# Emitting the first convolution of a state-space / attention kernel in a searched order, with engines chosen along with it

## Chip, cores, metric

One core of a Trainium2 chip. The metric is the device time of one execution in microseconds (us). All quoted runs are of the fast state, unless marked. Engines: PE is TensorE, DVE is VectorE, ACT is ScalarE, POOL is GpSimd.

## The reference

Four layers on `x` of 2048 x 512 in bf16: convolution, attention, the same convolution, the same attention, each behind a layer norm and with a residual.

```python
def _A_ref(u, A_re, A_im, B_re, B_im, C_re, C_im, log_dt, Dskip):   # cut
    P = jnp.exp((dt * A)[:, :, None] * l[None, None, :])            # 512 x 128 x 2048
    K = jnp.einsum("dn,dnl,dn->dl", Cc, P, dt * Bc).real            # the long kernel
    Yf = rfft(pad(u)) * rfft(pad(K))                                # length 4096
    return irfft(Yf)[..., :L] + u * Dskip

def _B_ref(x, wqkv, wo):     # cut: 32 heads of 16, 8 keys at distance 0, 2, .., 14
    attn = softmax(where(mask, q . k * scale, -1e9))
    return (attn . v) @ wo

x = x + _A_ref(_layernorm(x), ...);  x = x + _B_ref(_layernorm(x), wqkv, wo)
x = x + _A_ref(_layernorm(x), ...);  x = x + _B_ref(_layernorm(x), wqkv, wo)
```

## The kernel before

The long kernel `K` is contracted on PE from eight tables of powers, which DVE builds by doubling: two products and a sum for each level. Transforms are matmuls; between two of them data is turned (transposed), by DMA or by PE. In the first conv all this is emitted by hand. (Names in the profiles of a conv: `Ttab` and `Y2tab` are tables, `Z` the first half of a transform and `zt` its turned copy, `xc` or `sp_u` the spectrum of the input, `Kt` or `sp_k` that of the kernel, `pa` and `pb` their products, `vp` the inverse in PSUM and `VT` its copy, `X` the rows on which the layers work, handled in four quarters. In an attention layer `xn` is the normed input, `xnT` its turned copy, and `L` (in the code `Lf`) holds the terms of the softmax.)

```python
class Tables:                                   # cut
    def base(self, T, hc, x0=0, x1=2, levels=range(4)):
        for lev in levels:
            nc.vector.tensor_tensor(dst, src, mult(0), ALU.mult)       # products
            nc.vector.tensor_tensor(tb[...], src, mult(1), ALU.mult)
            nc.vector.tensor_tensor(d, d, tb[... ::-1 ...], ALU.add)   # the level's sum
    def high(self, T, hc):                      # the same once more, 128 x 2048

# kernel_and_first_conv: steps are lists of closures, `play` emits lists in turn
play(t[:2], ks[5:6], [store], ks[6:9], t[2:3], p[:2], v[:1], t[3:4], p[2:3], v[1:2], p[3:], v[2:], [fin],
     ks[9:], t[4:], [lambda: residual(dc)])     # t tables, ks kernel spectrum, p products, v inverses
```

The three later stages are already emitted in a listed order, with fixed engines:

```python
def sums():                                     # b_layer, softmax: three adds on DVE
    den = tree("sm_s", ALU.add, F32)
    nc.vector.reciprocal(rdb, den)
    nc.vector.tensor_tensor(Lf, Lf, spread(rdb), ALU.mult)

def mm(j=j, wide=wide, begin=True, fts=range(4)):   # b_layer, output block (cut)
    if begin:
        nc.tensor.matmul(ps, ident[:], X[:, j, :], start=True, stop=False)     # residual
    for ft in fts:
        nc.tensor.matmul(ps, box["oT"][...], wo_t[:, ft, :], start=False, stop=(ft == 3))
es.append(pl.op("A", 0.48, lambda ...: evac(...), a, ...))                     # copy on ACT
```

## Time and profile before

558.31 us median (557.58 to 560.0, 4 runs); the profiled execution has a span of 560.9 us. I cut it at seven events: the first table seed (36.3 us), the end of the last joined spectrum product of the first conv, the first q·k product of the first attention layer, the end of its last value product, the end of the last spectrum product of the second conv, the first q·k product of the second attention layer, the end of its last value product. Busy us of the three engines in each stage, from the view by windows:

| stage | length | PE | DVE | ACT |
|---|---|---|---|---|
| tables and first conv | 199.65 | 124.5 | 181.8 | 120.2 |
| entry to attention 1 | 17.87 | 13.8 | 14.3 | 11.9 |
| body of attention 1 | 103.40 | 94.6 | 92.8 | 59.1 |
| join and second conv | 64.27 | 55.7 | 46.7 | 58.4 |
| entry to attention 2 | 25.14 | 17.5 | 20.2 | 13.7 |
| body of attention 2 | 101.05 | 93.6 | 92.0 | 48.0 |
| tail | 13.20 | 8.2 | 0.0 | 4.9 |

Read it by asking which engine fills its row: DVE the first, PE and DVE the bodies, ACT (91%) the second conv. The lines themselves are in the prediction.

### The profile page before, as it was taken

The page shows a single profiled execution, that of the slowest core. Times are in us where ns is not written, and L with a number is a line of the kernel's source. Part 1 is how long each engine was busy: PE and PEld are TensorE (multiplying, and loading weights), DVE is VectorE, ACT ScalarE, POOL GpSimd, SP SyncE. Part 2 cuts the span into 40 slices and gives each one's busy share as a digit, 9 for nine tenths or more (in the row PEclk, how much of TensorE's full clock was granted, in tenths as well). Part 3 has the DMA queues.
Part 4 walks back from the last instruction along what each step waited for, and adds up shares of the span by engine and source line. Part 5 has one row for each costly group of instructions (what it writes and reads, how often), then busy time and mean ns, then how long its engine had stood idle before and what let it go on. Part 6 is the DMA issues. An engine that isn't in the chain of part 4 may idle for free.

```text
span 560.9 us, 11633 instructions
## 1 busy us (share of the span) xinstructions
PE 412.3 (74%) x4838; PEld 236.1 (42%) x4838; DVE 477.0 (85%) x805; ACT 343.8 (61%) x516; POOL 12.9 (2%) x62
## 2 busy tenths in 40 slices
PE   1201465585586678879999789868994998996996
PEld 0100333363454447543446234455763533552353
DVE  5999999999979959787799998537999587999890
ACT  4999765435355546865666147999974756642253
POOL 0000000000000001200000000000000000000000
PEclk9999998789799879999999799979998899998799
DMA  8200175646453474621010412615330500123141
GB/s 272 111 1 0 31 129 108 96 113 114 78 151 51 95 152 122 223 57 47 16 51 30 104 37 39 250 69 88 71 71 0 76 28 16 50 69 71 34 131 76
DMA packets 91808, 46.65 MB, mean 83 GB/s; under 512 B 80882, under 2 KB 87026, under 8 KB 90474
## 3 DMA queue, kind: packets, MB, share of 16 engines
q1 hardware_dynamic: 90170, 45.51, 34.2%
q8 instruction: 38, 0.62, 0.5%
q10 hardware_dynamic: 1584, 0.39, 0.3%
q14 instruction: 16, 0.13, 0.1%
HBM read 15.77 MB, written 8.13 MB: 43 GB/s over the span
## 4 chain that ended last, share of the span: by engine, by line
PE 38%; DVE 35%; ACT 14%; DMA 6%; issue 6%; SPq 1%; DVEq 0%; ACTq 0%
PE ps_qk L1072 8%; PE po L1232 5%; PE ps_v L1092 4%; DVE prod L1216 3%; PE Lp L1133 3%; DVE Ttab L579 3%; DMA zt<-Z 2%; PE ps_o L1286 2%; DVE ln_st_b L148 2%; DVE Ttab L547 2%; DVE Y2tab L579 2%; DVE prod L1123 2%; ACT Z L808 2%; DVE tb L544 2%; DVE Ttab L543 2%
## 5 line engine op out<-in xcount | busy, mean ns | idle before, releaser
L1123 DVE TENSOR_TENSOR prod<-qT,kT 128x2048 bf16<-128x2048 bf16 (+1 forms) x80 | 75.5, 1006 | 14.8 <-ACT kT L1077 8.7
L1216 DVE TENSOR_TENSOR prod<-VX,L 128x2048 bf16<-128x2048 bf16 (+2 forms) x96 | 77.0, 863 | 1.4 <-PE Lp L1133 0.9
L1232 PE MATMUL po<-prod,sb_ident 128*128 128x512 bf16 x224 | 59.0, 411 | 10.4 <-DVE prod L1216 9.5
L1072 PE MATMUL ps_qk<-xnT,wqk 128*128 128x512 bf16 x256 | 64.1, 385 | 3.1 <-ACT qT L1077 1.4
L213 PE MATMUL psA<-X,sb_F 128*128 128x128 bf16 x128 | 12.2, 238 | 43.3 <-ACT X L638 33.3
L213 PEld LDWEIGHTS <-sb_F 128*128 128x128 bf16 x256 | 19.0, 112 | 59.0 <-issue 58.1
L1232 PEld LDWEIGHTS <-sb_ident 128*128 128x128 bf16 x224 | 22.6, 104 | 41.1 <-issue 11.3
L1072 PEld LDWEIGHTS <-wqk 128*128 128x128 bf16 x256 | 22.7, 99 | 34.0 <-issue 14.2
L607 ACT CAST KTq<-psk 128x1024 bf16<-128x1024 f32 (+1 forms) x9 | 8.3, 917 | 42.5 <-PE psA L238 41.0
L1092 PE MATMUL ps_v<-wv,xnT 128*128 128x256 bf16 x256 | 33.2, 278 | 1.0 <-ACT xnT L1051 0.8
L216 ACT CAST Z<-psA 128x1024 bf16<-128x1024 f32 (+1 forms) x32 | 29.0, 970 | 8.0 <-PE psA L213 8.0
L597 PE MATMUL psk<-Ttab 128*32 128x64 bf16 x1024 | 22.5, 206 | 13.9 <-issue 13.9
L1077 ACT CAST qT<-ps_qk 128x512 bf16<-128x512 f32 x32 | 18.8, 588 | 18.0 <-PE ps_qk L1072 18.0
L1286 PE MATMUL ps_o<-wo_t,oT 128*128 128x512 bf16 x112 | 29.7, 386 | 0.0
L1252 ACT CAST ot<-po 128x1024 bf16<-128x1024 f32 x14 | 13.6, 1014 | 25.8 <-PE po L1232 25.8
L1133 PE MATMUL Lp<-prod,sb_bones 128*32 128x512 bf16 x256 | 28.1, 394 | 1.0 <-DVE prod L1123 0.8
L310 ACT CAST VT<-psA 128x512 bf16<-128x512 f32 x32 | 17.2, 589 | 17.5 <-PE psA L276 16.3
L1092 PEld LDWEIGHTS <-xnT 128*128 128x128 bf16 x256 | 23.8, 99 | 9.6 <-issue 4.5
L579 DVE TENSOR_TENSOR Ttab<-Ttab,MPA 128x2048 bf16<-128x2048 bf16 (+2 forms) x20 | 27.7, 1431 | 0.0
L1097 ACT CAST VX<-ps_v 128x512 bf16<-128x512 f32 x32 | 18.8, 587 | 14.3 <-PE ps_v L1092 14.3
L579 DVE TENSOR_TENSOR Y2tab<-Ttab,MPB 128x6144 bf16<-128x6144 bf16 (+1 forms) x13 | 27.2, 2119 | 0.0
L1077 ACT CAST kT<-ps_qk 128x512 bf16<-128x512 f32 x32 | 18.8, 587 | 11.7 <-PE ps_qk L1072 11.6
(203 smaller groups left out, 1018.0 us busy)
## 6 DMA issues: line engine op xcount, KB each, us to landing
X<-in_A_u_dram SPq DMA_DIRECT2D x8, 512.0 KB, 5.2
kt_scratch<-Kt SPq DMA_DIRECT2D x4, 1024.0 KB, 5.1
Kt<-kt_scratch SPq DMA_DIRECT2D x4, 1024.0 KB, 8.9
out_dram<-X SPq DMA_DIRECT2D x4, 512.0 KB, 2.7
k_scratch<-KTq SPq DMA_DIRECT2D x7, 256.0 KB, 2.4
KT<-k_scratch SPq DMA_DIRECT2D x7, 256.0 KB, 2.9
VX<-VX SPq DMA_DIRECT2D x4, 448.0 KB, 3.7
kT<-kT SPq DMA_DIRECT2D x8, 192.0 KB, 2.1
```

What stands on the lines that cost most here:

```text
L213: nc.tensor.matmul(o, F1[:, j, r, :], rhs_j(j), start=True, stop=not dk)
L216: nc.scalar.copy(Z[:, 0:n // 8, :, jq * 32:(jq + 1) * 32].rearrange("p g r k -> p r g k"), ps[:, :, 0:n // 8, :])
L579: nc.vector.tensor_tensor(dst, src.to_broadcast([128, q, n, 2 * EYB]), mm.to_broadcast([128, q * n, EYB, 2]), ALU.mult)
L597: nc.tensor.matmul(o.rearrange("e (s i) -> e s i", s=2), xs, T[:, 1:3, h, m // 2, :, t], start=(m == 0), stop=False, skip_group_check=True)
L1072: nc.tensor.matmul(ps[:], wqk[:, ct, f0:f0 + 128], xnT[:, 4 * s:4 * s + 4, ct, :], start=(ct == 0), stop=(ct == 3))
L1077: nc.scalar.copy((qT, kT)[which][fp][:, f2, o:o + 512], box.pop(("qk", which, fp, f2, s))[:])
L1092: nc.tensor.matmul(ps[:, jj].rearrange("p t h d -> p (t h d)"), xnT[:, j + jj, ct, :], wv[:, ct, fp * 256:(fp + 1) * 256], start=(ct == 0) ...
L1123: nc.vector.tensor_tensor(pr[:, 0:n2], qT[fp][:, a:a + n2, j0 * 128:j0 * 128 + 1024], kT[fp][:, a:a + n2, c0:c0 + 1024], ALU.mult)
L1133: nc.tensor.matmul(Lp[r0:r0 + 32, w // 4, :], bones[:, w % 4, :], pr[:, f2 - a, hb * 512:(hb + 1) * 512], start=(n == 1), stop=(n == 4), s ...
L1216: nc.vector.tensor_tensor(p2[:, 0:nj].rearrange("p j t d h -> p (j t) d h"), VX[:, fp, NV + a:NV + a + nj].rearrange("p j (t d h) -> p (j ...
L1232: nc.tensor.matmul(po[:, c:c + 512], ident[:], p2[:, k + j:k + j + 2].rearrange("p j t d h -> p (j t d h)"), start=(n == 1), stop=(n == W))
L1286: nc.tensor.matmul(ps, box["oT"][:, ft // 2, j, ft % 2, :], wo_t[:, ft, :], start=False, stop=(ft == 3))
```

## The change

The intent: write the first conv, too, as operations with dependencies, search an order for all engines together offline, and let the search choose the engine of small pieces of work. An operation may have two ways; the way whose numbers appear in the order is built.

```diff
+ORDERS = [ "33 58 34 59 35 60 36 61 37 62 ...",        # first conv: new; three more, all searched anew
 class Plan:
+    def either(self, name, *ways):
+        for k, way in enumerate(ways):
+            self.way = name, k
+            out.append(way())
     def run(self):
         order = [int(i) for i in ORDERS[Plan.turn].split()]
+        taken = {self.ops[i][2] for i in order}
+def moved(pl, nc, name, us, slow, fn, *after, **needs):   # a PSUM copy on ACT or on DVE
+    return pl.either(name, lambda: pl.op("A", us, lambda: fn(nc.scalar.copy), *after, **needs),
+                     lambda: pl.op("V", slow, lambda: fn(nc.vector.tensor_copy), *after, **needs))
+    def sum_mm(self, ps, ident, hc, lev, k):               # Tables: a sum as two matmuls with the identity
+            self.nc.tensor.matmul(o, ident, a[:, i * n:i * n + n], start=True, stop=False)
+            self.nc.tensor.matmul(o, ident, b[:, i * n:i * n + n], start=False, stop=True)
+        psA = es.enter_context(tc.tile_pool(name="k_psA", bufs=3, space=PSUM))      # was 2
+                t = pl.either(("turn", kind, dc, i), by_dma, by_pe) if both else by_dma()
+            return o, pl.either(("join", dc, c), lambda: [], lambda: pl.op("V", 0.7, join, o))
-                den = tree("sm_s", ALU.add, F32)
+                    for w in range(W):                      # softmax sums: eight matmuls into PSUM
+                        nc.tensor.matmul(ps[:], ident[:], Lf[:, :, w, :], start=(w == 0), stop=(w == W - 1))
+            a = pl.either(("den", fp, j0), on_tensor, on_vector)
+        def added(j, ps):                                   # output block: residual as an add on DVE
+            nc.vector.tensor_tensor(X[:, j, :], ps, X[:, j, :], ALU.add)
```

(Cut to its core. A "join" is the subtract and add that turn the two complex products into one spectrum on DVE; without it the inverse has 16 matmuls instead of 8.)

## The prediction

> **What bounds the kernel now.** I first read the engine totals and the 40 slices of the page, to see which engine is full where.
>
> ```profile
> PE 412.3 (74%) x4838; PEld 236.1 (42%) x4838; DVE 477.0 (85%) x805; ACT 343.8 (61%) x516; POOL 12.9 (2%) x62
> ...
> PE   1201465585586678879999789868994998996996
> ...
> DVE  5999999999979959787799998537999587999890
> ```
>
> No engine is full all the time: DVE (second row of digits) is full in the first third, where PE is half used, and PE is dense from the middle on. So I cut the span into stages and asked for the busy time of each engine in each stage (window, its length, then PE, weight loads, DVE, ACT, POOL, clock, DMA share):
>
> ```profile
> 36.00:236.00 200.00, 124.50 (x2875) 84.89 (x2874) 182.15 (x242) 120.51 (x158) 7.48 (x13) 0.91 0.48 100
> 236.00:250.00 14.00, 9.98 (x86) 6.12 (x87) 13.18 (x69) 8.92 (x18) 0.00 (x0) 1.00 0.27 67
> 250.00:345.00 95.00, 87.86 (x543) 40.56 (x542) 84.24 (x107) 50.23 (x79) 2.39 (x20) 0.96 0.19 47
> 345.00:425.00 80.00, 68.69 (x584) 45.34 (x583) 59.79 (x135) 72.23 (x121) 0.00 (x0) 0.96 0.40 100
> 440.00:548.00 108.00, 100.59 (x642) 47.16 (x641) 94.36 (x132) 53.84 (x80) 2.39 (x20) 0.95 0.23 57
> 548.00:561.00 13.00, 7.87 (x38) 3.29 (x35) 0.00 (x0) 4.69 (x8) 0.00 (x0) 0.94 0.21 82
> ```
>
> Four regimes. The tables and first conv (36 to 236 us) are DVE's: 182 of 200 us, PE and ACT near 60%. The bodies of the two attention layers (250 to 345, 440 to 548) are shared by PE (93%) and DVE (88%). The join of the first attention layer to the second conv and that conv (345 to 425) is ACT's, 90%. The last 13 us have no DVE at all: PE, then the last store.
>
> Next, the waits of DVE in the first window, because idle time of the bound engine is what an order can win:
>
> ```profile
> DVE pa L283 <- ACT Kt L239: 9.3, 4, 3.8
> DVE pa L283 <- issue: 2.7, 2, 2.2
> DVE pa L283 <- ACT X L329: 2.2, 1, 2.2
> ```
>
> 14.2 us, all before one instruction, the spectrum product: written in its place in program order, it stands at the head of DVE's queue while table work behind it could run. Last, the time order of one table sum, and the end of the chain of waits:
>
> ```profile
> 177.39 1.23 DVE L558 TENSOR_TENSOR Ttab<-Ttab,MHA 128x2048 bf16<-128x2048 bf16 x1
> 178.53 1.22 DVE L559 TENSOR_TENSOR tx<-Ttab,MHB 128x2048 bf16<-128x2048 bf16 x1
> 179.78 1.22 DVE L561 TENSOR_TENSOR Ttab<-Ttab,tx 128x2048 bf16<-128x2048 bf16 x1
> 180.93 3.42 DVE L579 TENSOR_TENSOR Ttab<-Ttab,MPA 128x2048 bf16<-128x2048 bf16 x2
> ```
>
> ```profile
> 529.88 3.45 PE po L1232 x16
> ...
> 554.62 0.22 PE ps_w L1284
> 554.84 0.45 PE ps_w L1286 x2
> 555.29 0.02 issue
> 555.31 0.59 ACT X L1414
> 555.90 0.04 issue
> 555.95 0.61 PE ps_w L1286 x2
> 556.55 0.02 issue
> 556.58 0.59 ACT X L1414
> ```
>
> Starts, not durations, count on DVE: L558 to L559 is 1.14 us, L559 to the dependent L561 1.25 us. In the tail every output block pays a 0.22 us residual matmul (L1284), and the last block waits for the copy of the one before.
>
> **What the Trainium skill says.** "VectorE: DVE Perf Modes", Side-by-side: where the cycles go for N=2048 bf16, gives about 1224 ns for a two-per-cycle operation; the trace has 1.22 us, so a table sum is already at its best rate and can only be moved. "TensorE: Matmul & The Clock Gate", Wait, 56ns, not 53.3ns?, gives a start-to-start of 215.7 ns at N=512 and 55.6 ns at N=128 once warm; 3.45 us over 16 matmuls is 0.216 us each, in agreement. "Perfetto Trace Analysis", Optimizing Scalar/DVE Operations, gives DVE a higher access overhead on PSUM than on SBUF, and ScalarE a lower one on PSUM. The trace agrees: 128x512 out of PSUM is 682 ns on DVE (VT, L881) and 588 ns on ACT (qT, L1077), so a copy given to DVE costs slightly more engine time than it saves on ACT. "PSUM — Partial Sum Buffer", Specifications (TRN2), allows a VectorE instruction one tensor from PSUM; the new add takes ps_o from PSUM and X from SBUF, so it is in order.
>
> **The change, part by part.** I counted the two built programs' instructions by engine, tile and size, and priced the difference with the durations above. Total counts hardly move (DVE 805 before and after), so this is a change of order and of engine.
>
> Tables and first conv. (a) Four of eight 128x2048 high sums and one 128x1024 sum leave DVE: 4 x 1.25 + 0.7 = -5.7 us DVE. They come back as 36 matmuls of N=512 (7.8 us PE) and 8 copies of 128x1024 plus 2 of 128x512 (8 x 1.02 + 2 x 0.59 = 9.3 us ACT), on engines at about 60%. (b) The first half table is no longer built in two halves: some -0.7 us. (c) Seven spectrum pairs are joined on DVE instead of four: 3 x 0.77 = +2.3 us; one VT copy +0.7. (d) Thirteen turns leave the DMA queue for PE and ACT (13 x 1.02 = 13.3 us ACT, about 6 us PE), which shortens the chain from Z to product; three PSUM buffers for two. DVE work: -5.7 - 0.7 + 2.3 + 0.7 = -3.4 us. ACT reaches some 143 of 200, PE some 136: neither becomes the bound. (e) In DVE's new list the products stand behind table work (table 5 is nearly done before the second group of products, and statistics fill the last spectrum's latency), so most of the 14.2 us should close; I take 10. Stage: -13 us.
>
> Entry of the first attention layer (236 to 250): PE waits for the norms there. DVE keeps its statistics; I take -1.
>
> Attention bodies. Seven of eight softmax sums go to PE: each takes 0.42 + 0.29 + 0.29 = 1.0 us off DVE, -7.0 us in all, and adds 8 matmuls of N=128, 0.45 us, 3.1 us PE in all. The waits of DVE for the exponential, 4.6 us in two waits, go because the list puts products between the steps. Fourteen q and k copies come to DVE (14 x 0.6 = +8.5) where it waited 14.5 us for them. Nineteen of 32 residual matmuls go (-19 x 0.216 = -4.1 us PE) and become adds on DVE (19 x 0.62 = +11.8, most in the tail and in the join where DVE is idle; about six within the second body). Four of eight turns of xn on PE go to DMA (-1.8 us PE). First body: DVE 84.2 - 3 + 3.7 = 85, PE about 89, of 95: the floor is near 89, and I take half of the room, -3. Second: DVE 94.4 - 4 + 4.9 + 3.7 = 99, PE about 101, of 108: I take -4.
>
> Join and second conv (345 to 425), ACT's. Quarter 2 goes to batch statistics: four squares with their reads, 4 x 0.92 = -3.7, four reads of the sum -0.8; five output copies become adds, -3.0; two more norms +1.6. In the conv: five 128x1024 and two 128x512 Z copies, three zt copies and one X copy leave (-5.3 - 1.2 - 3.1 - 0.6), thirteen VT copies arrive (+7.8). ACT: -8.3 us of 72. DVE takes some +4 us and has 20 us free. The rest is latency (a 5 us transposing DMA, a 10 us wait for the first xc), so I take 5 of the 8. Turn to the second layer (425 to 440): four norms leave DVE, -1.
>
> Tail. Eight output blocks after the last value product save 8 x 0.22 = 1.7 us, and the last block's wait for a copy goes, 0.6: -2.
>
> Sum: -13 - 1 - 3 - 4 - 5 - 1 - 2 = -29. The stages are not independent and a searched order meets real latencies, so I keep 26: 558.4 - 26 = **532 us**.
>
> **Rivals.** (1) Only the moved work counts and the idle time merely changes place: the offline order rests on durations that the chip does not keep, and DVE's queue is strict, so a late copy blocks as before. Then -3 in the first stage, -4 in the join, -2 in the tail, about nothing in the bodies: some 549 us. For it: the three later stages already had listed orders and still hold 20 us of DVE waits. Against it: the first stage was hand ordered and holds 14.2 us on one line. (2) The moves make ACT the bound in the first stage: 120 us rises by 23 to 143 of about 187, in bursts where sums, turns and copies meet; table sums would then wait on ACT and give the 5.7 us back. Against it, the new list puts two to four DVE operations behind each moved sum. Result near 541. (3) The order closes nearly everything: first stage 187 - 4, bodies at the floors 89 and 101, all 8 us of the join: about 520.
>
> **Range and chances.** I hold the centre at 532, between (2) and (3); 8 times in 10 it should be between 522 and 545, the upper end being half of the reordering lost. Faster by over 2% means under 547.2: only a full rival (1) misses it. 0.91 faster, 0.08 within 2%, 0.01 slower.
>
> **What would show it.** Right: the last joined product before about 223 us instead of 236; the waits of DVE before the products, 14.2 us, under 5; DVE busy in that stage about 179; no wait for the exponential; ACT in the join stage about 64; no residual matmul on the chain of waits in the last 8 blocks, and a chain that ends in a DVE add. Wrong: waits of DVE on the copies of moved sums, bodies still 95 and 108 us long, or a first stage over 195 us.

## The result

530.43 us median (529.37 to 532.08, 4 runs) against 558.31: ratio 0.9499, 95% interval 0.9466 to 0.9532. A ratio is the mean time of one kernel's fast runs over that of the other's fast runs in the same rounds, so it is not quite the ratio of the medians. The profiled execution has a span of 528.9 us, 32.0 us less than the one of before (medians: 27.9). The profiled execution of the kernel before took 562.7 us by the device's clock, more than any of its four timed runs, so the changes by stage below are together some 4 us too large. A later set of runs on a chip where the kernel before took 560.2 us gave 529.6 us and 0.9456.

The page of the changed kernel, engine totals and DVE's 40 slices:

```profile
PE 404.1 (76%) x4929; PEld 238.6 (45%) x4943; DVE 475.5 (90%) x803; ACT 339.2 (64%) x505; POOL 12.9 (2%) x62
...
DVE  4999999999999998749899998889989497999995
```

DVE's busy time hardly moved (477.0 to 475.5 us): it is the same work in a shorter span. The digits of the first conv (fourth to sixteenth slice) are now 9s but for the last. The stages (window, length, busy PE, weight loads, DVE, ACT, POOL, clock, DMA share):

```profile
36.55:216.38 179.83, 127.32 (x2990) 90.20 (x2991) 176.04 (x246) 139.13 (x186) 7.47 (x13) 0.94 0.39 93
216.38:237.21 20.83, 14.55 (x100) 8.92 (x100) 10.44 (x56) 13.04 (x23) 0.00 (x0) 0.84 0.45 85
237.21:335.36 98.15, 89.79 (x594) 43.07 (x598) 91.45 (x124) 51.55 (x83) 2.39 (x20) 1.00 0.21 46
335.36:392.40 57.04, 52.02 (x456) 35.22 (x456) 50.99 (x112) 52.36 (x88) 0.00 (x0) 1.00 0.66 144
...
417.24:517.16 99.92, 91.44 (x608) 43.87 (x613) 94.93 (x127) 39.51 (x55) 2.39 (x20) 1.00 0.22 56
```

| stage | before | after | change | predicted | after, second profile |
|---|---|---|---|---|---|
| tables and first conv | 199.65 | 179.83 | -19.8 | -13 | 179.33 |
| entry to attention 1 | 17.87 | 20.83 | +3.0 | -1 | 20.28 |
| body of attention 1 | 103.40 | 98.15 | -5.3 | -3 | 98.15 |
| join and second conv | 64.27 | 57.04 | -7.2 | -5 | 57.10 |
| entry to attention 2 | 25.14 | 24.84 | -0.3 | -1 | 24.74 |
| body of attention 2 | 101.05 | 99.92 | -1.1 | -4 | 100.19 |
| tail | 13.20 | 11.74 | -1.5 | -2 | 11.73 |

The last column is from the control run below. The experiments are read by stages, so what counts is how well an unedited stage repeats. Over all profiles with the changed kernel's code in a stage, the second conv stays within 57.0 to 57.1 us, the second body within 99.9 to 100.2, the tail within 11.7 to 12.1, the first stage within 179.3 to 179.8; the first body is 98.1 to 98.2 us, but 99.4 in experiment 3; the entries vary more, the first from 20.2 to 20.8 us (to 23.3 behind an edited first stage), the second from 23.4 to 24.9. So the -0.3 us of the second entry is within its spread. Experiment 1, which keeps the old later stages, gives a second value for them too: 103.4, 64.1, 24.4, 100.1 and 13.0 us. Against these the second body gains only 0.2 us.

The waits of DVE in the first stage, 14.2 us before, are 2.4 us:

```profile
DVE ln_st_b L150 <- ACT X L856: 1.4, 2, 0.9
DVE Ttab L480 <- ACT Ttab L525: 0.8, 1, 0.8
DVE pa L802 <- ACT sp_k L738: 0.2, 1, 0.2
```

And the chain of waits ends in matmuls and a DVE add in place of residual matmuls and an ACT copy:

```profile
523.91 0.61 PE ps_w L1426 x2
524.52 0.02 issue
524.54 0.69 DVE X L1409
```

**Where the first stage's 19.8 us came from.** I took the start and duration of each of DVE's instructions in this stage from the trace and sorted what lies between the end of one and the start of the next: listed waits, small positive gaps, and overlaps (the next starts before the end of the one before). With the durations they add up to the stage:

| us | listed waits | small gaps (number) | overlaps (number) | durations | sum |
|---|---|---|---|---|---|
| before | 14.2 | 3.6 (88) | -12.0 (143) | 193.8 | 199.6 |
| after | 2.4 | 1.4 (37) | -17.5 (202) | 193.5 | 179.8 |
| change | -11.8 | -2.2 | -5.5 | -0.2 | -19.8 |

So 11.8 us are closed waits; another 7.8 us (before rounding) come from how an instruction starts behind the one in front. In the changed kernel's order list, 37 of DVE's 142 steps follow directly on a step whose result they need, the same number as the small gaps. Of these gaps, 35 are about 0.03 us long, while the overlaps are 0.09 us on average. That the durations fell by only 0.2 us in sum is because sixteen of the layer norm's statistics, with durations of 4.5 us, moved in from the entry.

### The profile page after: what moved, and what is told of

Read it like the earlier page. It is cut to its first block, busy times and chain, and to the rows that moved or that the text cites. A ratio compares the mean times of both kernels' runs of the same rounds, so it can differ in the third digit from the quotient of the medians.

```text
span 528.9 us, 11855 instructions
## 1 busy us (share of the span) xinstructions
PE 404.1 (76%) x4929; PEld 238.6 (45%) x4943; DVE 475.5 (90%) x803; ACT 339.2 (64%) x505; POOL 12.9 (2%) x62
## 4 chain that ended last, share of the span: by engine, by line
PE 34%; DVE 33%; ACT 10%; issue 9%; DMA 3%; SPq 0%; POOL 0%; DVEq 0%; ACTq 0%
PE ps_qk L1190 11%; DVE prod L1353 7%; PE ps_v L1210 4%; PE Lp L1251 3%; DVE Y2tab L545 3%; DVE Ttab L545 3%; DVE ln_st_b L150 2%; DVE Ttab L488 2%; DVE Ttab L481 2%; DMA Kt<-kt_scratch 2%; DVE Ttab L480 2%; PE ps_o L1426 2%; DVE prod L1241 2%; ACT X L598 1%; PE po L1374 1%
## 5 line engine op out<-in xcount | busy, mean ns | idle before, releaser
L1241 DVE TENSOR_TENSOR prod<-qT,kT 128x2048 bf16<-128x2048 bf16 (+1 forms) x80 | 77.1, 1005 | 15.7 <-ACT kT L1195 15.0
L1369 PE MATMUL po<-prod,sb_ident 128*128 128x512 bf16 x216 | 54.5, 378 | 8.1 <-DVE prod L1353 4.9
L1369 PEld LDWEIGHTS <-sb_ident 128*128 128x128 bf16 x224 | 21.4, 97 | 35.6 <-issue 11.7
L520 PE MATMUL ps_sum<-Ttab,sb_ident 128*128 128x512 bf16 x18 | 8.3, 459 | 31.0 <-DVE Ttab L480 27.7
L716 ACT CAST Z<-ps_s 128x1024 bf16<-128x1024 f32 (+1 forms) x32 | 29.4, 995 | 0.5 <-PE ps_s L711 0.4
L561 PE MATMUL psk<-Y2tab,Ttab 128*32 128x48 bf16 x1024 | 21.5, 198 | 9.5 <-issue 8.5
L1426 PE MATMUL ps_o<-wo_t,oT 128*128 128x512 bf16 x108 | 27.5, 379 | 0.3 <-issue 0.2
L1195 ACT CAST qT<-ps_qk 128x512 bf16<-128x512 f32 x24 | 14.0, 584 | 19.4 <-PE ps_qk L1190 19.4
L150 DVE BATCH_NORM_STATS2 ln_st_b<-X 128x6 f32<-128x128 bf16 (+2 forms) x80 | 22.9, 355 | 3.7 <-ACT X L856 3.3
L1195 ACT CAST kT<-ps_qk 128x512 bf16<-128x512 f32 x26 | 15.2, 584 | 16.5 <-PE ps_qk L1190 16.5
L558 PEld LDWEIGHTS <-Ttab 128*32 128x32 bf16 x1024 | 19.4, 102 | 13.1 <-issue 12.2
```

Source lines behind the costliest of these rows:

```text
L150: self.nc.vector.bn_stats(self.st[:, j, part, :], X[:, j, a:b])
L558: nc.tensor.matmul(o.rearrange("e (s i) -> e s i", s=2), xs, T[:, 1:3, h, m // 2, :, t], start=(m == 0), stop=False, skip_group_check=True)
L716: nc.scalar.copy(box["Z", kind, dc][:, 0:n // 8, :, jq * 32:(jq + 1) * 32].rearrange("p g r k -> p r g k"), box.pop(("s1", kind, dc, jq))[ ...
L1195: copy((qT, kT)[which][fp][:, f2, o:o + 512], box.pop(("qk", which, fp, f2, s))[:])
L1241: nc.vector.tensor_tensor(pr[:, 0:n2], qT[fp][:, a:a + n2, j0 * 128:j0 * 128 + 1024], kT[fp][:, a:a + n2, c0:c0 + 1024], ALU.mult)
L1369: nc.tensor.matmul(po[:, c:c + 512], ident[:], p2[:, k + j:k + j + 2].rearrange("p j t d h -> p (j t d h)"), start=(n == 1), stop=(n == W))
```

## Experiments

All kernels gave the correct result. The kernel before took 560.2 to 560.7 us on the chips of these runs, so I compare ratios and stage lengths. Except for the first and the eleventh, an experiment edits only the order lists (an alternative way is taken by its numbers appearing). No order was searched anew after a choice had been undone, so a loss below is the loss in this order, not what the choice is worth against an order of its own. The third PSUM buffer was not undone in any run. Line numbers in the experiments' profiles are lower than in the changed kernel (L749 there is L802 here).

### 1. The new first stage alone

```diff
-def kernel_and_first_conv(...)      # hand order
+def kernel_and_first_convF(...)     # the changed kernel's, with its Tables, Plan and first order; all else as before
```

> The kernel before with only its tables and first conv replaced by those of the changed kernel; the other three orders and all later engine choices are the old ones. The profile of the changed kernel puts -19.8 us on that stage (199.7 to 179.8 us, from the first table seed to the last joined product) and +3.0 us on the entry to the first attention layer (17.9 to 20.8 us). Theory A, the entry loss belongs to the new order of the first attention layer: this kernel has the short stage of about 180 us and an entry of at most 17.9 us, so about 558.3 - 19.8 = 538.5 us, down to 536 if the 13 statistics that now lie inside the stage (2.6 us) shorten the entry as well. Rival B, the entry loss comes from the way in which the new first stage ends: entry near 21 us and about 541.5 us. Later stages should stay within 1 us of the kernel before.

542.21 us, ratio 0.9683. Stage 179.3 us; entry 20.0 us; later stages 103.4, 64.1, 24.4, 100.1 and 13.0 us, each within 1 us of before. The first stage is worth its 20 us by itself. The entry, though, is 2.1 us longer than before under the old order of attention 1, so theory A falls: most of the entry's loss comes with the new first stage. (I had counted thirteen statistics as moved; it is sixteen.) In both kernels the first copy of a quarter of X starts 3.0 us after the last joined product, but the old conv hands over quarter 0 first and the new one quarters 2, 1, 0, 3, while the old attention layer begins with quarter 0: DVE waits 3.3 us for it.

### 2. Table sums back on DVE

```diff
-... 5 67 57 ...    -... 89 78 21 ... 15 79 76 16 ... 91 77 92 ...     # PE sums, ACT copies
+... 5 65 57 ...    +... 89 21 ... 15 16 ... 91 75 92 ...              # one DVE add each; five sums in all
```

> The changed kernel with the five table sums that moved to TensorE and ACT (four of 128x2048, one of 128x1024) back on DVE, the rest of the order kept. Theory A, the stage is bound by DVE's work: 4 x 1.25 + 0.7 = 5.7 us more, stage 179.8 to about 185.5 us and the kernel 530.4 to about 536 us. Rival B, the order hides it (DVE had that much idle time in the stage): within 1 us of 530.4 us.

534.14 us, ratio 0.9535; stage 183.1 us, +3.2. DVE's durations rose by 5.0 us, but the adds also fill places: a listed wait of 0.8 us for the copies goes, and there are ten more overlaps. The moved sums are worth 3.2 of the 19.8 us, some two thirds of their work.

### 3. Contiguous tables

```diff
-33 58 34 59 35 60 36 61 37 62 38 63 39 64 40 ...
+33 58 34 35 36 37 38 39 40 43 44 59 60 ...        # likewise for all eight tables
```

> The changed kernel, the same instructions on the same engines, only DVE's order in the first stage is altered: in each of the eight tables the seed and the products and sums of the four levels stand directly behind each other instead of having other tables' work between them. In the changed kernel 37 of 142 steps of DVE's list follow directly on the step that they depend on; here 73. Theory A, a DVE instruction that reads what the one just before it wrote starts some 0.12 us later than an independent one (in the traces a gap of +0.03 us in place of an overlap of 0.09 us), and the profile lists no wait for it: 36 x 0.12 = 4.3 us more, stage about 184 us, kernel about 534.7 us, with the listed waits of DVE in the stage still near 2.4 us. Rival B, such gaps cost nothing in sum: within 1 us of 530.4 us. If the listed waits grow by several us, the test is spoilt for the total and only the count of small gaps says something.

542.02 us, ratio 0.9682; stage 192.3 us, +12.5. Small gaps 37 to 72, overlaps 202 to 159: +1.6 and +4.3 us. But listed waits also grew by 6.5 us, so the total is spoilt as a test, as the expectation allowed. Hence experiment 7.

### 4. The order without the choices

```diff
 # in the first order
-22 times the way that the search took: 5 sums, 11 turns, 5 joins, 1 VT copy
+22 times the way of the kernel before, at the same place in the list
```

> The changed kernel's order in the first stage, with the engine choices of the kernel before: all table sums on DVE, joins only for the last quarter of the channels, all but two of the turns by DMA, every VT copy on ACT (22 choices undone; the third PSUM buffer stays). Theory A, the order closes the waits and gaps and the choices are worth only their DVE work: +5.7 us of sums, -2.3 us of three joins, -0.7 us of a VT copy = +2.7 us, stage about 182.5 us, kernel about 533 us. Rival B, the order only works with the choices it was searched with: turns by DMA (some 5 us each) come later than the order supposes and DVE waits for products again, over 8 us of listed waits before the products, stage over 190 us and kernel over 540 us.

554.01 us, ratio 0.9893. The stage is 203.2 us: 3.5 us longer than in hand order, and theory A is wrong by 20 us. DVE's largest waits in this stage, of 22.9 us in all:

```profile
DVE pa L749 <- PE vp L773: 8.9, 2, 7.0
DVE ln_st_b L150 <- ACT X L803: 7.7, 3, 4.4
DVE pa L749 <- ACT sp_k L685: 4.3, 2, 3.3
```

Products wait for their buffers (the inverse on PE still reads them) and for the kernel's spectrum (its turn), statistics for X. DVE's own starts stay good (34 small gaps, 200 overlaps): that part of the gain belongs to the order. The closed waits do not; they need the other engines to deliver when the order supposes.

### 5. Turns by DMA

```diff
-... 146 135 111 147 192 136 150 114 151 ...      # transposes on PE, copy on ACT
+... 146 134 111 147 192 149 114 ...              # one transposing DMA each; 11 in all
```

> The changed kernel with only the turns of the first conv put back: 11 of the 13 that moved to TensorE and ACT go by DMA again, the order kept. The order with all choices undone gave a first stage of 203.2 us instead of 179.8, with 22.9 us of listed DVE waits, of which 8.9 us before a product for a buffer that the inverse still read, 7.7 us before statistics for X, 4.3 us before a product for the kernel's spectrum. Theory A, the order needs the turns on TensorE: the chain from Z to the spectrum grows by some 3 to 4 us per turn, the waits for X and for the spectrum come back (10 us or more), stage over 189 us. Rival B, it was the unjoined products that blocked: stage within 3 us of 179.8 us and listed waits under 5 us.

542.57 us, ratio 0.9677; stage 190.9 us, +11.0, listed waits 13.2 us. Theory A.

### 6. Joins off

```diff
-... 622 567 557 ... 617 569 630 ... 582 575 583 577 431 ...   # joins of the third quarter of the channels
+... 622 568 557 ... 617 630 ... 582 576 584 431 ...           # 16-matmul inverses; one other join added
```

> The changed kernel with only the joins of the first conv put back as before: the four of the third quarter of the channels are no longer joined on DVE (each inverse has 16 instead of 8 matmuls), the third one of the last quarter is joined. DVE work falls by 3 x 0.77 = 2.3 us. Theory A of the run before this one (turns decide): stage 177.5 to 181 us. Rival B (unjoined products hold the two pa buffers while the inverse takes twice as long on TensorE): the wait of products for PE vp returns with 6 us or more and the stage is over 185 us.

536.25 us, ratio 0.9564; stage 185.1 us, +5.2, although DVE has 3.3 us less to do. DVE's listed waits are 9.7 us instead of 2.4: that of products for PE's inverse is 2.9 us, not 6, and statistics wait 3.3 us for X. Neither theory is right alone: here both choices are needed, and undoing turns costs twice as much as undoing joins.

### 7. Sums right behind their products

```diff
-35 60 36 61 37 62 38 63 ...
+35 36 60 61 37 38 62 63 ...      # 19 sums, each moved up by one or two places
```

> The changed kernel, the same instructions on the same engines; 19 table sums in DVE's list are moved up by one or two places, so that they stand directly behind the products that they add. 53 of 142 steps follow directly on the one that they depend on, instead of 37; no product moves by more than one place, so no other wait should change by much. Theory A (a dependent start costs about 0.12 to 0.15 us more than an independent one, unlisted): 16 x 0.12 to 0.15 = 1.9 to 2.4 us, stage about 181.9 us, kernel about 0.4% slower than the changed one. Rival B (the larger loss with contiguous tables was all waits): stage within 0.5 us of 179.8 us.

532.03 us, ratio 0.9491; stage 181.7 us, +1.85; small gaps 37 to 52, overlaps 202 to 188; listed waits 2.2 us as before. Theory A: the starts cost 2.5 us more (gaps +0.8, overlaps +1.7), shorter durations and waits give 0.6 back, so 0.12 to 0.17 us for each of the fifteen. (Against the control's stage of 179.3 us the loss is 2.3 us. The ratio is not above the changed kernel's first one; beside the control's 0.9456 it is 0.4% higher, but the intervals, up to 0.9479 and from 0.9466, touch, so it is the stage that shows the loss, not the total.) The same place in the changed kernel, then here, time line of DVE (start, duration, instruction):

```profile
158.87 1.22 DVE L481 TENSOR_TENSOR Ttab<-Ttab,MUB 128x2048 bf16<-128x2048 bf16 x1
160.00 0.22 DVE L456 COPY Ttab<-cb 128x128 bf16<-128x128 bf16 x1
160.12 1.23 DVE L488 TENSOR_TENSOR Ttab<-Ttab 128x2048 bf16<-128x2048 bf16 x1
```

```profile
159.20 1.22 DVE L428 TENSOR_TENSOR Ttab<-Ttab,MUB 128x2048 bf16<-128x2048 bf16 x1
160.45 1.22 DVE L435 TENSOR_TENSOR Ttab<-Ttab 128x2048 bf16<-128x2048 bf16 x1
161.60 0.21 DVE L403 COPY Ttab<-cb 128x128 bf16<-128x128 bf16 x1
```

The sum starts 1.25 us after the product that it needs in both. In the changed kernel the copy of the next table's seed fits into that time; in the experiment it comes after the sum, and takes its own.

### 8. First quarter first

```diff
 # end of the first order: quarters 2, 1, 0, 3 become 0, 1, 2, 3
-... 699 696 700 693 697 702 694 703
+... 693 696 694 699 697 702 700 703
 # start of the second order: statistics 0 and 1, norms 0 and 1, then 2 and 3; q·k projections before values
-39 20 40 1 21 22 41 2 58 3 23 59 42 4 30 10 ...
+1 2 20 21 3 4 5 7 13 14 9 11 16 17 22 23 24 26 ...
```

> The changed kernel with another entry to the first attention layer: the first conv hands over its quarters of X in the order 0, 1, 2, 3 instead of 2, 1, 0, 3; DVE takes the statistics of quarters 0 and 1, then the norms of quarter 0 (all four on DVE, none on ACT) and quarter 1, and only then the statistics of quarters 2 and 3; TensorE projects what the first products need before anything else. Same work but for two norms. Theory A, the entry became longer (17.9 to 20.8 us) because TensorE waits 4.7 us for the first norm, then runs its first 24 matmuls at half speed (8 matmuls of ps_v in 1.89 us, 1.05 before), and projects other things first: TensorE's wait falls to about 2 us, ps_v to about 1.05 us, the entry to 16 to 17.5 us and the kernel by 3 to 4 us to about 527 us. Rival B, TensorE has a fixed amount of projections to do before DVE can go on, so DVE's time is only lost a little later: the entry is shorter but the body of the first attention layer (98.2 us) longer by the same, kernel within 1 us of 530.4 us.

528.09 us, ratio 0.942 (0.9395 to 0.9446); entry 18.1 us, body 99.0 us. PE at the entry, in the kernel before and in the changed one:

```profile
243.09 1.27 PE L1048 MATMUL pt_x<-sb_ident,xn 128*128 128x128 bf16 x16 [1.99 <-DVE xn L182]
244.90 1.05 PE L1092 MATMUL ps_v<-wv,xnT 128*128 128x256 bf16 x8 [0.54 <-ACT xnT L1051]
```

```profile
226.11 1.89 PE L1165 MATMUL pt_x<-sb_ident,xn 128*128 128x128 bf16 x16 [4.74 <-ACT xn L1154]
228.30 1.89 PE L1210 MATMUL ps_v<-wv,xnT 128*128 128x256 bf16 x8 [0.31 <-ACT xnT L1168]
```

In the changed kernel PE waits 4.7 us for the first norm, and its next 24 matmuls are slower (16 transposes 1.89 us for 1.27, eight of ps_v 1.89 for 1.05): the granted clock is 0.50 from 223.9 to 230.7 us, and 1.00 in the whole entry of the kernel before. In the experiment the wait before the transposes is 1.8 us, and ps_v takes 1.04 us again, but a second wait of 1.4 us lies before the projections, whose first sixteen matmuls took 5.2 us (the next sixteen, 3.6), with a granted clock of 0.50 from 225.5 to 228.9 us. Theory A in part: 2.2 us shorter than the control's entry, of which the body gives 0.9 back. By stages the edit is worth 1.3 us; the control's interval (0.9433 to 0.9479) touches this one's, so as a total it is not proved. It is the one version here that may beat both kernels.

### 9. Softmax sums on DVE, second conv's copies on ACT

```diff
 # second and fourth order, seven places: eight matmuls become three DVE adds
-... 271 290 156 277 291 163 ...
+... 271 292 293 294 156 277 295 163 ...
 # third order, eleven places: PSUM copy on DVE becomes PSUM copy on ACT
-... 22 19 26 ... 34 111 106 ...
+... 22 18 26 ... 34 110 106 ...
```

> The changed kernel with two engine choices undone in stages that can be read apart, orders kept. (1) All seven softmax sums that moved to TensorE are back on DVE (three adds each, some 1.0 us; three in the first attention layer, four in the second); the waits for ps_den (0.8 and 2.4 us) go with them. (2) In the second conv the eleven copies out of PSUM that moved to DVE (five of 128x1024, six of 128x512) are back on ACT, 5 x 1.02 + 6 x 0.59 = 8.6 us of ACT. Theory A for (1), DVE is full there: bodies 98.2 + 3.0 = 101.2 us less at most the 0.8 us wait, and 99.9 + 4.0 - 2.4 = 101.5 us. Rival B, DVE has the room (6.7 and 5.0 us idle in the bodies): both within 0.5 us of 98.2 and 99.9. Theory A for (2), the stage is bound by ACT: 57.0 + about 8.6 = 64 to 66 us, which is the whole gain of that stage. Rival B, its gain came from the join's statistics and adds: under 60 us.

538.72 us, ratio 0.9616. Bodies 100.3 and 102.3 us: +2.1 and, against the control's 100.2, +2.1. Theory A of (1). Second conv 61.7 us, +4.6 against the control's 57.1: between the two theories of (2). DVE's largest wait there, none of which the changed kernel has (before: 10.0 us):

```profile
DVE pa L993 <- ACT xc L982: 16.5, 5, 11.3
```

### 10. q and k copies on ACT, residuals of the tail on PE

```diff
-... 229 112 113 ...   88 115 248 ...      # copy on DVE (way 1); 6 + 8 places
+... 229 111 113 ...   88 114 248 ...      # copy on ACT (way 0)
-output blocks 8 to 11 and 13 to 15 of the last layer: 4 matmuls, add on DVE
+output blocks 8 to 11 and 13 to 15 of the last layer: residual matmul first, copy on ACT
```

> The changed kernel with two other choices undone, orders kept. (1) The 14 copies of q and k that moved to DVE (six in the first, eight in the second attention layer) are back on ACT: DVE loses 4.1 and 5.5 us of work, ACT gains 3.5 and 4.7 us. Theory A, the copies belong on DVE because it waits for kT and qT anyway: bodies within 1 us of 98.2 and 99.9 us, or longer. Rival B, they only load the fuller engine: bodies shorter by 2 us or more each. (2) The seven output blocks of the tail (8 to 11, 13 to 15 of the last layer) get their residual matmul on TensorE and the copy on ACT again: by the prediction 7 x 0.216 + 0.6 us, so a tail of 11.8 + 2.1 = 13.9 us; if the tail is set by the last store alone, 11.8 to 12.3 us.

531.63 us, ratio 0.9501. Bodies 99.7 and 100.0 us: +1.5, and within 0.3 us of both profiles of the changed kernel. Theory A: the copies cost nothing on DVE, and in the first body they seem to help (one profile; the unedited body was 99.4 us once, in experiment 3). Tail 12.9 us, +1.1 where 2.1 was expected.

### 11. Both entries

```diff
 # a_layer: statistics of the first three channel groups only for quarters 0 and 1
-pl.op("V", 1.95, lambda: ln_b.gather(X, 0, j0, j0 + 4), a)
+pl.op("V", 1.95, lambda: None if q > 1 else ln_b.gather(X, 0, j0, j0 + 4), a)
 # b_layer, start(q): the others here
+if part == 1 and q > 1:
+    ln_b.gather(X, 0, j0, j1)
 # third and fourth order: quarters 0, 1, 2, 3; statistics and norms of 0 and 1 first (and experiment 8)
```

> The entry of the run with the first quarter first (18.1 us in place of 20.8, body 0.9 us longer, kernel about 1.0% better than the changed one by the ratios), and the same idea at the entry to the second attention layer (24.8 us): the second conv hands over quarters 0, 1, 2, 3 in this order; only the first two quarters have their statistics of the first three channel groups taken before (4 instead of 8 us of DVE work ahead of the first norm), those of the last two are taken after the norms of the first two; TensorE has projections and values of the first two quarters to do meanwhile. Same work but for two norms. Theory A, TensorE's wait of 6.2 us for the first norm falls to about 2 us and the entry by 3 to 5 us, of which the body gives 1 us back: kernel 2 to 4 us under the run with the first quarter first. Rival B, the products need the keys of the last two quarters right after the first two products, and these come no earlier: entry shorter but body longer by the same, no gain.

534.05 us, ratio 0.9542: worse than experiment 8. Entry 25.5 us (control 24.7), body 104.8 us (control 100.2). PE did start earlier (wait 1.8 us), but after its first eight projection matmuls it waits again, 3.1 us, and sixteen of them run at 0.45 us each instead of 0.22. In the body DVE waits 4.0 us for projections that now come late. Rival B, and worse than it.

### 12. The changed kernel again

No edit; the control.

> The changed kernel itself, unaltered, on the same chip and in the same rounds as the run with both entries, as the control for it. Ratio to the kernel before 0.947 to 0.953; first stage 179.8 us, entries 20.8 and 23.5 to 24.8 us, bodies 98.2 and 99.9 us, second conv 57.0 us, tail 11.8 us.

529.60 us, ratio 0.9456 (0.9433 to 0.9479). Stages as in the table above. The ratio is just under the expected range, on a chip where the kernel before is slower; the entry to attention 1, 20.3 us, is 0.6 us shorter than in the first profile, with a granted clock of 0.92 instead of 0.84.

## Why the prediction was right, and where it was not

The total was right: 532 predicted, 530.4 measured, 28 us less in place of 26. Of its signs, the last joined product ends at 216 us (before 223), DVE is busy 176 us in that stage (179), no wait for the exponential is listed (but see the bodies), no residual matmul stands on the chain at the end, and that chain ends in a DVE add. By steps:

- **First stage, bound by DVE.** Right that it is DVE's, and rival (2), ACT as the new bound, did not happen: ACT is busy 139 of 180 us and DVE waits 0.8 us for copies of moved sums. Work: -3.4 predicted; measured -0.2 with 4.5 us of statistics added, so about -4.7. Waits: 10 us to close predicted, 11.8 measured. The term that was missing is the start of a dependent instruction. The prediction saw it ("L559 to the dependent L561 1.25 us" against 1.14) and priced it for four moved sums only; the order changes it at some fifty places and wins 7.8 us. Experiment 7 measures it by itself: 1.85 us for fifteen.
- **Why the waits close.** Here the step failed although its size was nearly right. The prediction gave them to the order ("products stand behind table work") and let the turns merely shorten a chain. Experiment 4: the same order without the choices leaves 22.9 us of waits, and the stage is longer than by hand. Undone singly, turns cost 11.0 us, joins 5.2, sums 3.2; undone together (with one VT copy), 23.3. The joins I had counted as a cost, +2.3 us of DVE: without them DVE waits 7.3 us more, 2.9 of them for a buffer of the products that PE still reads, so they are worth 5.2 net. That 10 us came so near to 11.8 is partly luck.
- **Entry to attention 1.** Wrong in sign: -1 predicted, +3.0 (control +2.4) measured, although 3.2 us of statistics left it: before, they filled DVE's time until the first X came. What grew is the way to the first norm on DVE, which starts 6.3 us after the last joined product before, 7.7 in experiment 1, 8.7 in the changed kernel and 6.4 in experiment 8, with entries of 17.9, 20.0, 20.8 and 18.1 us. In experiment 1 the conv hands over its quarters in an order that does not suit the old layer; in the changed kernel DVE takes the statistics of all four quarters before its first norm, in experiment 8 those of two. PE's longer wait then costs it its clock (0.84 in this stage, 1.00 before); what that alone costs was not measured.
- **Bodies.** -3 and -4 predicted, -5.3 and -1.1 measured (the second only -0.2 against experiment 1). Softmax sums on PE are worth 2.1 us in each (experiment 9). The failed part is "the waits of DVE for the exponential go": in the second body the 2.4 us wait only changed its releaser, a wait in place of the one removed:

```profile
DVE sm_rdb L1322 <- PE ps_den L1334: 2.4, 1, 2.4
```

  In the first body it fell from 2.2 to 0.8 us. The q and k copies on DVE, priced at work against waits with no gain, give 1.5 us in the first body and nothing in the second (experiment 10). The rest of the difference between the bodies, among it the six adds on DVE in the second, was not tried singly.
- **Join and second conv.** -5 of ACT's 8.3 us predicted, -7.2 measured; ACT's busy time there fell by 6.0 us (58.4 to 52.4). Eleven copies moved to DVE are worth 4.6 us (experiment 9): without them the 10 us wait for xc, which the prediction took for latency, is there again, larger. The other 2.6 us (statistics, adds) were not tried singly.
- **Tail.** -2 predicted, -1.5 measured. Residual matmuls and the copy wait were priced at 2.1 us for the seven blocks tried; putting them back cost 1.1. Not every residual matmul was on the path.
- **Entry to attention 2.** -1 predicted, -0.3 measured, within the spread of that stage.
- **A reading.** "The trace agrees", of access overheads, says too much: 682 and 588 ns compare DVE and ACT on PSUM, and no number there compares SBUF with PSUM.

The entry's error and the second body's were made up by the first stage and the second conv. The mechanism of the total stands; it was right as a sum whose parts missed by up to 7 us, and that they cancelled is luck.

## What to carry to other kernels

An order and the engine choices that it was searched with are one change: price the choices by when they deliver to the bound engine, not by the work they add. On an engine that is full, look at starts as well as at waits and durations: the profile lists no wait for an instruction that needs the result of the one in front of it. Where a searched stage meets the next one, check the order in which its results arrive against the order in which they are used.

## What the Trainium skill lacked or had wrong

- "VectorE: DVE Perf Modes", The DRAIN you can't avoid: eight copies took 13.88 us with a semaphore after each and with one after the last, so "the semaphore costs nothing extra here", and its Rules for kernel authors say to minimise the number of operations, not of semaphores. Here an instruction that needs the result of the one in front of it starts some 0.12 us later than one that does not (1.25 against 1.14 us after a 128x2048 product), and with the same instructions, fifteen more such places took 1.85 us. The page lacks this case, and I found no figure for it in the other pages.
- "TensorE: Matmul & The Clock Gate", Part 1: The HAM clock gate, puts the fall to half clock at one idle window or more of about 3.4 us, free-running. The trace agrees in that eight matmuls of ps_v took 1.89 us after waits of 4.7 us (changed kernel) and 3.5 us (experiment 1), and 1.05 us after waits of 2.0 and 0.5 us (kernel before). It differs in the time of the fall. In the changed kernel the granted clock is 0.99 from 221.4 to 223.9 us and 0.50 from there to 230.7; in experiment 11 it is 1.00 from 396.9 to 399.4 us and 0.50 from there to 413.1. Both times it fell some 2.5 us after the last matmul before PE's wait, less than a whole window. In experiment 11 that was 0.8 us into 16 transposes behind a wait of only 1.8 us, and eight projection matmuls then ran at 0.45 us instead of 0.22; whether transposes count as work for the clock was not tested here.
